# The second Fourier outer product split in seven and moved behind the seventh, in a fused attention and Fourier kernel

## The chip, the cores and the metric

One Trainium2 chip, one core. The metric is the device time of one execution in microseconds, from three runs of each kernel; a profile comes from one further execution. The engines are called PE (TensorE), DVE (VectorE), ACT (ScalarE), POOL (GpSimd) and SP (SyncE, which here only issues transfers).

## The reference

Two independent branches, joined along the last axis: multi-head attention with 32 heads of 32, and a Fourier mixing layer written as matrix products, all in float32.

```python
qkv = (A_x @ wqkv)                                  # 2048 x 1024 by 1024 x 3072, 32 heads
p = softmax(einsum("bhqd,bhkd->bhqk", q, k) * Dh ** -0.5)
a = concat_heads(einsum("bhqk,bhkd->bhqd", p, v)) @ wo
u = einsum("bsd,ed->bse", B_x, dft_hid_re)          # likewise with dft_hid_im
y = einsum("ts,bse->bte", dft_seq_re, u) - einsum("ts,bse->bte", dft_seq_im, u_im)
return concatenate([a, y], axis=-1)
```

## The kernel before

**Products.** Every large product is done by a Strassen-like scheme: operands are cut in quarters, and seven products of sums of quarters replace eight. The products are numbered 1 to 7, and p means such a number. Each operand is kept as a high and a low float32r part (`halves`: a cast at line 549 or 550, a subtraction at line 553), and a pair of 128 x 128 weights and 128 x 512 moving tile takes three matmuls: high by high, low by high, high by low. All of them are recorded at line 433, in `group` (the first ones at line 455).

**Stages.** In program order of these product matmuls: the projections to q, k and v (2016 matmuls); the first Fourier step along the sequence, `dense1` (seven outer products, 2592 here); the second Fourier step, `dense2` (1344); the output projection, `project` (672), which needs all heads.

**The outer products of dense1.** They run in the order `OUTER`, here 1, 2, 5, 6, 7, 4, 3. A plain one (`simple`) has four column blocks n, and for each four row blocks m, and each of the 16 groups adds up 8 pairs: 16 x 8 x 3 = 384 matmuls. Its weights are held for all four n: those of m = 0 and 1 in tiles h and l, those of m = 2 and 3 in slots 16 to 19. A product named in `SPLIT` (here 1 and 3) is itself done in seven inner products, in the order `WITHIN`, by `split`: 7 x 4 groups of 4 pairs, 7 x 4 x 4 x 3 = 336 matmuls. It has more sums of quarters to make (`fetch`: loads at lines 511 and 520, additions at line 530, stores of sums used again at line 538), and it gathers its inner products in accumulators, which lie in slots 16 to 19 (lines 1115 and 1117). `inner` ends its results; for any product but the first, a partial result of another product is loaded (line 1107) and added (line 1141) before the result is stored (line 994, `put_out`). A plain product gathers with a loaded partial result (line 1205) in one instruction at line 986.

**Attention.** Each head has score matmuls psS (line 1586) for the row maxima (DVE, line 1592) and sums (ACT, line 1595), transposed score matmuls psT (line 1711) with an exponential on ACT (line 1718), and the second product P V (line 1741). The maxima's row of a head goes out to DRAM and back by SP (lines 1633 and 1634: m_d, then into qs) before its transposed scores can run.

**What sets the order.** A planner (`Plan`) with costs per operation writes out one fixed order for every engine when the program is built. It hands out product matmuls ("fills") beside attention work: a fill goes when no attention work can, or when its paid share lags behind the attention's done share. Fills of a split product weigh HEAVY = 1.5, and in their stretch (`spare`) ACT may take casts.

```python
        for p in OUTER:
            heavy[0] = HEAVY if p in SPLIT else 1.0
            spare[0] = p in SPLIT
            split(p) if p in SPLIT else simple(p)
```

## Time and profile before

| | us |
|---|---|
| median of three runs | 2923.82 (2922.07 to 2924.57) |
| the profiled execution | 2924.82 |
| its span | 2923.0 |
| TensorE busy | 2911.5 |
| VectorE busy | 2260.2 |
| ScalarE busy | 2297.2 |
| GpSimd busy | 1107.2 |

Times of instructions below are from the profiled execution and counted from the start of its span. A matmul's record lasts longer than its slot (0.39 us), since matmuls overlap; what one costs is the distance between starts. Stretches of outer products are taken by the product matmuls' count in the fixed order: product 1 from 782.2 us, then 2 from 947.8, 5 from 1143.1, 6 from 1340.4, 7 from 1535.6, 4 from 1732.1, 3 from 1928.2, and the second Fourier step from 2108.3 to the end of attention near 2762.2. "x" before a count is the number of instructions; in tables by stretch the columns are stretch, its length, and then for PE, its weight loads, DVE, ACT and POOL the busy time with the count.

### The profile page before, as it was taken

Reading aid. Unit: us, or ns where it says so; the run is one execution under the profiler, and the core shown is the slowest. Engines: PE = TensorE matmul, PEld = TensorE weight load, DVE = VectorE, ACT = ScalarE, POOL = GpSimd, SP = SyncE. Lnnn points to the kernel's source line nnn. Section 1 sums busy time; section 2 is a strip of 40 time slices with the busy share of each in tenths; the row PEclk is TensorE's granted clock in tenths of the full one; section 3 lists DMA queues with packets and bytes.
Section 4 is the critical chain, followed back from the end, with each engine's and each line's share of the span. In section 5 each row is a group of like instructions: output and inputs, shape, how many; then the busy total and the mean of one; then the engine's idle time right before and its main releaser. Section 6 shows DMA issues by size and latency. Waiting matters only on the chain.

```text
span 2923.0 us, 46116 instructions
## 1 busy us (share of the span) xinstructions
PE 2911.5 (100%) x14826; PEld 2130.8 (73%) x14826; DVE 2260.2 (77%) x3072; ACT 2297.2 (79%) x4369; POOL 1107.2 (38%) x866
## 2 busy tenths in 40 slices
PE   9999999999999999999999999999999999999999
PEld 7887777776667776777776777777677777777787
DVE  7778888788889768777778787778877877876496
ACT  5348888888899888888888888988888888887532
POOL 2323335222365124243434342347613653342042
PEclk9999999999999999999999999999999999999999
DMA  9975658766687448678869775568735776663463
GB/s 340 372 241 186 201 183 280 231 214 223 220 263 227 146 136 274 219 241 273 277 224 286 227 240 170 155 192 281 231 98 172 255 238 189 188 189 123 124 241 140
DMA packets 444956, 636.24 MB, mean 218 GB/s; under 512 B 115726, under 2 KB 150286, under 8 KB 444590
## 3 DMA queue, kind: packets, MB, share of 16 engines
q1 hardware_dynamic: 444716, 633.29, 67.8%
q8 instruction: 120, 1.97, 0.3%
q14 instruction: 120, 0.98, 0.1%
HBM read 448.56 MB, written 184.57 MB: 217 GB/s over the span
## 4 chain that ended last, share of the span: by engine, by line
PE 94%; ACT 2%; DMA 2%; DVE 1%; issue 1%; SPq 0%; DVEq 0%; ACTq 0%
PE pd L433 43%; PE psT L1711 16%; PE psS L1586 15%; PE pd L1741 14%; PE psT L433 6%; ACT psS L1595 1%; ACT pt L1718 1%; DMA qs<-m_d 0%; DMA m_d<-lt 0%; DVE negm L1592 0%; DMA raw<-in_ct 0%; PE psT L455 0%; DMA er<-in_xa 0%; DMA qs<-qk_d 0%; DMA er<-in_wv 0%
## 5 line engine op out<-in xcount | busy, mean ns | idle before, releaser
L1592 DVE TENSOR_REDUCE negm<-psS 128x1 f32<-128x1024 f32 x1024 | 1242.4, 1220 | 255.9 <-PE psS L1586 244.6
L1595 ACT ACTIVATE psS<-psS,negm 128x1024 f32<-128x1024 f32 x1024 | 1230.0, 1201 | 75.2 <-DVE negm L1592 69.5
L1718 ACT ACTIVATE pt<-psT 128x512 f32<-128x512 f32 x1656 | 1000.8, 705 | 267.4 <-PE psT L1711 243.8
L433 PE MATMUL pd<-slot,h 128*128 128x512 f32 x2704 | 921.3, 390 | 0.0
L1711 PE MATMUL psT<-qs,ks 128*128 128x512 f32 x2048 | 794.5, 394 | 2.3 <-ACT pt L1718 1.3
L553 POOL TENSOR_TENSOR slot<-raw,slot 128x512 fp32r<-128x512 f32 x278 | 357.6, 1292 | 776.1 <-DVE slot L550 424.2
L433 PEld LDWEIGHTS pd<-slot,h 128*128 128x128 f32 x2704 | 507.5, 188 | 106.1 <-issue 0.8
L530 POOL TENSOR_TENSOR raw<-raw,g 128x512 f32<-128x512 f32 x321 | 414.8, 1302 | 428.4 <-issue 78.1
L433 PE MATMUL pd<-slot,l 128*128 128x512 f32 x1352 | 526.7, 390 | 0.0
L1711 PEld LDWEIGHTS psT<-qs,ks 128*128 128x128 f32 x2048 | 381.9, 188 | 142.0 <-issue 42.7
L1586 PE MATMUL psS<-ks,qs 128*128 128x512 f32 x1552 | 474.0, 391 | 2.5 <-ACT psS L1595 2.2
L433 PE MATMUL pd<-slot,slot 128*128 128x512 f32 x1560 | 436.3, 389 | 0.0
L1741 PE MATMUL pd<-pt,vt 128*32 128x512 f32 x3312 | 408.2, 594 | 0.0
L1586 PEld LDWEIGHTS psS<-ks,qs 128*128 128x128 f32 x1552 | 290.0, 188 | 67.0 <-ACT psS L1595 6.2
L433 PEld LDWEIGHTS pd<-slot,slot 128*128 128x128 f32 x1560 | 292.8, 188 | 60.8
L1595 ACT ACTIVATION_READ_ACCUMULATOR psS<-psS,negm 128x1 f32 x1024 | 328.2, 321 | 0.0
L433 PEld LDWEIGHTS pd<-slot,l 128*128 128x128 f32 x1352 | 253.8, 188 | 52.3
L1718 ACT ACTIVATE ptm<-psT 128x512 f32<-128x512 f32 x392 | 242.4, 716 | 48.9 <-PE psT L1711 47.1
L1741 PEld LDWEIGHTS pd<-pt,vt 128*32 128x32 f32 x3312 | 108.6, 110 | 231.8 <-issue 217.2
L553 POOL TENSOR_TENSOR l<-raw,h 128x512 fp32r<-128x512 f32 x105 | 135.5, 1290 | 224.5 <-PE psT L1711 79.0
L550 DVE CAST slot<-raw 128x512 fp32r<-128x512 f32 x364 | 168.0, 482 | 6.2 <-DMA raw<-in_wo 3.1
L1586 PE MATMUL psS<-ks,qx 128*128 128x512 f32 x496 | 150.1, 393 | 1.0 <-ACT psS L1595 1.0
(158 smaller groups left out, 2066.0 us busy)
## 6 DMA issues: line engine op xcount, KB each, us to landing
raw<-in_ct SPq DMA_DIRECT2D x212, 256.0 KB
g<-in_ct SPq DMA_DIRECT2D x148, 256.0 KB
raw<-ut_d SPq DMA_DIRECT2D x112, 256.0 KB
qk_d<-e SPq DMA_DIRECT2D x52, 512.0 KB
qs<-qk_d SPq DMA_DIRECT2D x128, 192.0 KB
ks<-qk_d SPq DMA_DIRECT2D x128, 192.0 KB
c<-xx_d SPq DMA_DIRECT2D x80, 256.0 KB
c<-u_d SPq DMA_DIRECT2D x72, 256.0 KB
```

Of the source, the lines that this page charges most:

```text
L433: nc.tensor.matmul(box["ps"], a[1]((a[0].hi, a[0].lo)[u]()), b[1]((b[0].hi, b[0].lo)[v]()), start=k == 0, stop=k == n - 1)
L530: return (nc.gpsimd if e == "POOL" else nc.vector).tensor_tensor(out=dest(), in0=x, in1=y, op=ALU.add if sign > 0 and not turned else ALU. ...
L550: return nc.vector.tensor_copy(hi(), raw())
L553: return (nc.gpsimd if e == "POOL" else nc.vector).tensor_tensor(out=lo(), in0=raw(), in1=f(hi()), op=ALU.subtract)
L1586: nc.tensor.matmul(p[:, i * NB : i * NB + NB], (QX[0] if own else QS[h % 2])[:, qt * P : qt * P + P], KS[h % 2][:, c * 1024 + i * NB : c * ...
L1592: nc.vector.tensor_reduce(out=ST["negm"][:, c, qt : qt + 1], in_=box["p"], axis=AX.X, op=ALU.max, negate=True)
L1595: nc.scalar.activation(box["p"], box["p"], AF.Exp, bias=ST["negm"][:, c, qt : qt + 1], accum_out=ST["sums"][:, c, qt : qt + 1])
L1711: nc.tensor.matmul(box["p"], KS[h % 2][:, t * P : t * P + P], QS[h % 2][:, j * NB : j * NB + NB], start=True, stop=True)
L1718: nc.scalar.activation(box["t"], box["p"], AF.Exp)
L1741: nc.tensor.matmul(po["p"][j * DH : j * DH + DH, :], VT[h][:, k, :], box["t"], start=(k == t0), stop=(k == t), tile_position=(0, j * DH),)
```

## The change

The second outer product joins those that are split, and it comes behind the seventh in the order. The constant that tells the planner how many fills there are follows from the length of `SPLIT`.

```diff
@@ -391,7 +391,7 @@
-    SPLIT = (1,3)
+    SPLIT = (1,2,3)
     HEAVY = 1.5
     FILL = 3 * (7 * 24 * 4 + 7 * 16 * 8 - 16 * len(SPLIT) + 7 * 8 * 8 + 2 * 8 * 4)
@@ -1187,7 +1187,7 @@
-    OUTER = (1,2,5,6,7,4,3)
+    OUTER = (1,5,6,7,2,4,3)
     WITHIN = (1, 2, 5, 6, 7, 3, 4)
```

Three places of the fixed order show what moves. The first is PE behind product 7. Before, product 4 begins there: the number behind slot_ names a moving tile, 19472 is the last of the first group's eight, and 19069 is the first again, for the second group (qs and ks belong to scores, pt and ptm to P V).

```order
L433 MATMUL pd<-slot_19472,h 128x512
L1586 MATMUL psS<-ks_333,qx 128x512 x2
L1741 MATMUL pd<-ptm,vt 32x512 x4
L1741 MATMUL pd<-pt,vt 32x512 x23
L1741 MATMUL pd<-ptm,vt 32x512 x5
L1711 MATMUL psT<-qs_2580,ks_2581 128x512 x2
L1586 MATMUL psS<-ks_333,qx 128x512 x4
L1711 MATMUL psT<-qs_2580,ks_2581 128x512
L433 MATMUL pd<-slot_19472,l 128x512
L1711 MATMUL psT<-qs_2580,ks_2581 128x512
L433 MATMUL pd<-slot_19472,h 128x512
L433 MATMUL pd<-slot_19069,h 128x512
```

Now product 2 begins there, and PE's rows at the same turn from the first group to the second are these (17124 and 17171 are the third and fourth of four moving tiles, 17058 the first).

```order
L433 MATMUL pd<-slot_17124,h 128x512
L1586 MATMUL psS<-ks_2601,qs_2600 128x512 x2
L433 MATMUL pd<-slot_17124,l 128x512
L1711 MATMUL psT<-qs_332,ks_333 128x512
L433 MATMUL pd<-slot_17124,h 128x512
L1711 MATMUL psT<-qs_332,ks_333 128x512
L433 MATMUL pd<-slot_17171,h 128x512
L433 MATMUL pd<-slot_17171,l 128x512
L433 MATMUL pd<-slot_17171,h 128x512
L433 MATMUL pd<-slot_17058,h 128x512
L1586 MATMUL psS<-ks_2601,qs_2600 128x512 x2
L1711 MATMUL psT<-qs_332,ks_333 128x512
```

A group there has four pairs instead of eight, and attention's rows stand between them in the same way. The second place is DVE in product 2's stretch. Before, between the maxima of line 1592, it ends one group with one instruction (c is a partial result that was loaded).

```order
L1592 TENSOR_REDUCE negm<-psS 128x1
L986 TENSOR_TENSOR e<-c,pd 128x512
L1592 TENSOR_REDUCE negm<-psS 128x1
L550 CAST slot_11470<-raw 128x512
L553 TENSOR_TENSOR slot_11470<-raw,slot_11470 128x512
L1592 TENSOR_REDUCE negm<-psS 128x1 x3
L986 TENSOR_TENSOR e<-c,pd 128x512
L1592 TENSOR_REDUCE negm<-psS 128x1 x5
L986 TENSOR_TENSOR e<-c,pd 128x512
L1592 TENSOR_REDUCE negm<-psS 128x1
```

Now DVE in product 2's stretch, at its third inner product by WITHIN's numbers 5 and 6 (slot_17596 and slot_18259 are accumulators).

```order
L1592 TENSOR_REDUCE negm<-psS 128x1
L1117 TENSOR_TENSOR slot_17596<-slot_17596,pd 128x512
L1117 TENSOR_TENSOR slot_18259<-slot_18259,pd 128x512
L1592 TENSOR_REDUCE negm<-psS 128x1 x2
L1117 TENSOR_TENSOR slot_17596<-slot_17596,pd 128x512
L1117 TENSOR_TENSOR slot_18259<-slot_18259,pd 128x512
L1592 TENSOR_REDUCE negm<-psS 128x1 x2
L550 CAST slot_18613<-raw 128x512
L550 CAST slot_18618<-raw 128x512
L530 TENSOR_TENSOR raw<-raw,g 128x512
```

One group of such an inner product is added into two accumulators, and more casts stand between the maxima. The third place is SP's queue where the maxima's row of one head goes out (in product 7's stretch before, in product 2's now) (m_d_178, lines 1633 and 1634). Before, stores of results that DVE alone makes stand around it.

```order
L520 DMA g<-in_ct 128x512 x2
L538 DMA s_d_0_372<-raw 128x512
L520 DMA g<-in_ct 128x512
L1633 DMA m_d_178<-lt 4x32x32
L994 DMA ut_d_2_1_314<-e 128x4x128
L994 DMA xx_d_2_7_433<-e 128x512
L1634 DMA qs_332<-m_d_178 2x2048
L1205 DMA c<-xx_d_2_6_464 128x512
```

Now SP has these rows around the same head's row.

```order
L994 DMA ut_d_2_0_305<-e 128x4x128
L1107 DMA c<-xx_d_2_1_414 128x512
L511 DMA raw<-in_xb 128x512
L511 DMA raw<-in_ct 128x512
L994 DMA ut_d_2_0_305<-e 128x4x128
L1107 DMA c<-xx_d_2_1_430 128x512
L511 DMA raw<-in_ct 128x512
L1633 DMA m_d_178<-lt 4x32x32
L520 DMA g<-in_ct 128x512
L1634 DMA qs_332<-m_d_178 2x2048
```

The stores at line 994 are now of the split product's results, which POOL or DVE has first added to a partial result at line 1141, and the loads at line 1107 are those partial results.

## Rows read from the trace of the kernel before

**Rows 1.** The page: span, busy shares by engine, granted clock in 40 slices.
```profile
span 2923.0 us, 46116 instructions
PE 2911.5 (100%) x14826; PEld 2130.8 (73%) x14826; DVE 2260.2 (77%) x3072; ACT 2297.2 (79%) x4369; POOL 1107.2 (38%) x866
...
PEclk9999999999999999999999999999999999999999
```

**Rows 2.** Waits of PE: line waited for, us in total, times, longest.
```profile
PE psS L1586 <- ACT psS L1595: 3.2, 9, 0.6
...
PE psT L1711 <- ACT pt L1718: 1.3, 2, 1.1
PE psT L1711 <- DMA qs<-m_d: 0.8, 2, 0.5
```

**Rows 3.** The page: chain that ended last, shares by engine.
```profile
PE 94%; ACT 2%; DMA 2%; DVE 1%; issue 1%; SPq 0%; DVEq 0%; ACTq 0%
```

**Rows 4.** The chain in order of time: start, us, what; around attention's end.
```profile
2755.22 7.00 PE pd L1741 x64
2762.22 4.53 PE pd L433 x19
...
2769.47 5.44 PE pd L433 x24
```

**Rows 5.** Groups by line and shape: count, busy us, mean ns, idle before by releaser.
```profile
L1718 ACT ACTIVATE pt<-psT 128x512 f32<-128x512 f32 x1656 | 1000.8, 705 | 267.4 <-PE psT L1711 243.8 <-PE pd L1741 23.0
...
L553 POOL TENSOR_TENSOR slot<-raw,slot 128x512 fp32r<-128x512 f32 x278 | 357.6, 1292 | 776.1 <-DVE slot L550 424.2 <-DVE slot L553 72.8 <-PE pd L433 72.6
...
L550 DVE CAST slot<-raw 128x512 fp32r<-128x512 f32 x364 | 168.0, 482 | 6.2 <-DMA raw<-in_wo 3.1 <-POOL raw L530 1.2 <-DMA raw<-in_ct 0.9
...
L553 DVE TENSOR_TENSOR slot<-raw,slot 128x512 fp32r<-128x512 f32 x158 | 113.2, 732 | 8.4 <-ACT slot L549 7.6
...
...
L549 ACT ACTIVATE slot<-raw 128x512 fp32r<-128x512 f32 x72 | 47.8, 686 | 70.5 <-DVE raw L530 24.5 <-PE psT L433 20.3 <-DMA raw<-o_d 18.0
...
L1117 DVE TENSOR_TENSOR slot<-slot,pd 128x512 f32<-128x512 f32 x32 | 21.1, 681 | 3.2 <-PE pd L433 2.8
L1141 POOL TENSOR_TENSOR e<-e,c 128x512 f32<-128x512 f32 x15 | 19.4, 1294 | 8.6 <-DVE slot L550 7.8 <-DVE e L990 0.7
```

**Rows 6.** By stretch, all engines: products 1, 2, 5, 6, 7, 4, 3, dense2.
```profile
782.20:947.80 165.60, 164.44 (x840) 118.69 (x839) 145.07 (x208) 151.72 (x293) 105.83 (x84) 1.00 0.78 242
947.80:1143.10 195.30, 195.02 (x1019) 140.01 (x1018) 143.85 (x190) 165.10 (x319) 48.68 (x38) 1.00 0.57 172
1143.10:1340.40 197.30, 197.19 (x1030) 142.31 (x1029) 145.69 (x191) 169.20 (x326) 76.78 (x61) 1.00 0.72 232
1340.40:1535.60 195.20, 194.71 (x1021) 140.71 (x1020) 151.13 (x204) 166.04 (x320) 75.04 (x60) 1.00 0.82 266
1535.60:1732.10 196.50, 195.73 (x1021) 140.06 (x1020) 157.22 (x205) 166.40 (x319) 75.23 (x58) 1.00 0.79 248
1732.10:1928.20 196.10, 196.10 (x1026) 141.85 (x1026) 146.35 (x197) 169.04 (x326) 53.72 (x42) 1.00 0.57 171
1928.20:2108.30 180.10, 178.77 (x941) 125.34 (x941) 151.47 (x208) 158.13 (x306) 118.91 (x94) 1.00 0.81 254
2108.30:2762.20 653.90, 653.06 (x3418) 467.69 (x3416) 478.35 (x667) 530.22 (x1016) 247.79 (x194) 1.00 0.57 174
```

**Rows 7.** The same, P V (line 1741) on PE alone; products 1 and 2.
```profile
782.20:947.80 165.60, 26.79 (x240) 1.00 0.78 242
947.80:1143.10 195.30, 35.37 (x320) 1.00 0.57 172
```

**Rows 8.** The chain's shares by line in the stretches of products 4 and 3.
```profile
by line: PE pd L433 44.3%; PE psT L1711 19.3%; PE psS L1586 18.6%; PE pd L1741 17.9%
...
by line: PE pd L433 34.7%; PE pd L1741 19.4%; PE psS L1586 15.5%; PE psT L1711 15.0%; ACT psS L1595 8.7%; ACT pt L1718 4.3%; issue 1.6%; DVE negm L1592 0.7%; ACT ptm L1718 0.2%; DVE lh L1622 0.1%; DVE tt L1648 0.1%
```

**Rows 9.** Waits of the SP queue in product 3's stretch: us, times, longest.
```profile
SPq L994 <- POOL e L1141: 17.7, 9, 6.8
```

## Prediction

> **What bounds the kernel now.** I read the page's busy shares first, then who TensorE waited for, then the chain of waits, then tables by stretch. TensorE is busy 2911.5 of 2923.0 us, at the full granted clock in every slice [rows 1]. Busy time of matmuls is modelled, so three other views have to confirm it. Its waits: the longest group is 3.2 us in 9 waits, and behind it, beside start-up, come 1.3 and 0.8 us [rows 2]. The chain that ended last is 94% TensorE [rows 3]. And in order of time 24 matmuls of a product take 5.44 us, so one is worth 5.44/24 = 0.2267 us from start to start; 64 records of the second attention product (P V) take 7.00 us, 0.1094 us each [rows 4]. With these prices the content of the whole program is known: 6624 product matmuls and 2 x 2048 score matmuls at 0.2267, 4096 P V records at 0.1094, which is 1501.7 + 928.6 + 448.1 = 2878 us. Only 2923 - 2878 = 45 us is anything else, start and end included. So the kernel is bound by the number of its matmuls, and a matmul taken out is worth nearly its whole slot, unless the work that replaces it makes TensorE wait.
>
> The attention of the 32 heads and the Fourier products are interleaved on TensorE; only when the last head is done can the output projection begin. The last P V starts at 2755.22 us and 19 matmuls of the last Fourier step follow it at 2762.22 [rows 4]; then comes the projection.
>
> **What the change removes.** A plain outer product is 16 groups of 8 chunk pairs with 3 matmuls each, 384; one split in seven is 7 x 4 groups of 4 pairs, 336. The order agrees: 6552 rows of line 433 before, 6504 now, and 2048 of each attention kind in both; the runs of P V matmuls are 72 in both. That is 48 matmuls x 0.2267 = **10.9 us** of TensorE.
>
> By the Trainium skill (TensorE: Matmul & The Clock Gate, Back-to-back issue gap) such matmuls in a stream of weight loads and matmuls come 131 ns apart, and the 48 would be worth 6.3 us. The trace has 227 ns for one, over stretches of 24, and the measurement decides.
>
> **What it adds, beside TensorE.** The order has 20 more accumulations on DVE at lines 1115 and 1117 (0.68 us: 13.6 us), 13 more casts there (0.48: 6.3) and 13 more additions and subtractions (0.73: 9.5); 17 more casts on ACT (0.69: 11.7); on POOL 32 more at line 530, 25 at line 553 and 17 at line 1141 (1.29 each, as at the last two: 95.5 us); and 90 more transfers of 256 KB on SP's queue, 23 MB more beside 633 [rows 5]. The product's stretch is where this must fit. In the plain second product's stretch DVE is busy 143.85 of 195.3 us, ACT 165.10, POOL 48.68; in the third, already split, DVE 151.47 of 180.1, ACT 158.13, POOL 118.91 [rows 6]. So all of it fits: POOL has 61 us left there, DVE 28 and ACT 22. I cost it at nothing as busy time. Its cover is the stream of score and product matmuls; if DVE had to carry a further 28 us in that stretch, the maxima of the scores would come late and TensorE would wait for the score banks.
>
> **What it costs TensorE in waits.** This price can be read, since two products are split already. From each stretch of [rows 6] I take the content: its matmul count less the P V records at 0.2267, plus those (240 in product 1's and 320 in each of the others, [rows 7]) at 0.1094. Product 1 (split): 600 and 240, 162.3 us, and 165.6 were spent: 3.3 over. Product 3 (split): 621 and 320, 175.8 of 180.1: 4.3 over. The plain ones: product 2, 193.5 of 195.3, 1.8; product 5, 196.0 of 197.3, 1.3; product 6, 193.9 of 195.2, 1.3; product 7, 193.9 of 196.5, 2.6; product 4, 195.1 of 196.1, 1.0. The plain mean is 1.6 (part of it is the turn to P V and back). So splitting costs 3.3 - 1.6 = 1.7 us after product 1's pattern and 4.3 - 1.6 = **2.7 us** after product 3's. I take the latter, the nearer row: the new one, like product 3, adds a stored partial result on POOL behind each of its 16 final results (line 1141), which product 1 does not. The chain shows where it comes from: in product 3's stretch 8.7% and 4.3% of it run over ACT's two exponentials, in product 4's stretch it is all TensorE [rows 8].
>
> The moves. Product 5 now follows a split product, as product 2 did. Product 4 does so too, and there the held weights of its third and fourth row blocks (slots 16 to 19) can only be written when the accumulators in the same slots are read out for the last time. The first two row blocks, 48 matmuls among attention work, stand ahead and hide that. The only such row is product 2 with 1.8 over, beside 1.3 for product 5: **0.5 us** more, since now two products stand there rather than one. The other scatter among plain products, 1.0 to 2.6, has no cause that I can name, and I carry it as the error. The tail is unchanged in the order: 19 product matmuls behind the last P V in both programs, and the projection of 672 matmuls.
>
> **Sum.** -10.9 + 2.7 + 0.5 = -7.7 us. The profiled execution took 2924.82 us around a span of 2923.0, so 1.8 lie around the span and it was 1.0 above the median of the three runs, 2923.82. The span becomes 2915.3, that execution would be 2917.1, and the median 2916.1, 0.26% less. About 0.2%, 5.8 us, is what a measurement of this kernel can tell from no change. The surcharge may be between nothing (then the 10.9 stands whole: 2912.9; a gain from the new order itself I limit to the plain stretches' scatter) and double product 3's (5.4).
>
> **Rivals.**
> *Two split products near each other cost double.* Products 2 and 3 now have one plain product between them. If POOL's and ACT's backlogs pass over, each shows another surcharge: 2.7 + 2.7 + 0.5 = 5.9 against 10.9, so -5.0 and 2918.8, too little to be told from nothing. For it: the chain over ACT in product 3's stretch [rows 8]. Against: product 4's stretch between them is the quietest of all, POOL 53.72 of 196.1 us busy and 1.0 over content [rows 6].
>
> *TensorE has room, and the freed slots stay empty.* Then the end of attention is set by the engines beside it (ACT 79% busy, [rows 1]), the Fourier work is only done earlier, and the projection begins when it began: 2923.8, no change. Against: TensorE hardly waits for anybody [rows 2], ACT's idle time is mostly waiting for score matmuls, 243.8 us at line 1718 [rows 5], and the order still has Fourier matmuls up to the last P V. The Trainium skill speaks for this rival (Perfetto Trace Analysis, Identifying the Most-Contended Engine): it calls matmul busy time a poor measure and asks for the weight loads' busy share. That is 73% here [rows 1], which would leave a quarter of TensorE free; the back-to-back starts of [rows 4] contradict it.
>
> *The SP queue holds up a head.* Each result of the new product is stored from SP's queue behind POOL's addition, and the queue stands while it waits: 17.7 us in 9 waits, up to 6.8, in product 3's stretch [rows 9]. In the order the row of a head's maxima (lines 1633 and 1634), for which its transposed score matmuls wait, stands right behind such stores in the new stretch, where the order before has stores that wait for DVE alone. TensorE waited only 0.8 us on it so far [rows 2]. If all 17.7 us fell on head starts, the sum would be -10.9 + 2.7 + 0.5 + 17.7 = +10.0, or 2933.8. It turns to a loss once 7.7 us of it reaches TensorE.
>
> That the change does not do what it says is excluded by the order's counts.
>
> **How the numbers follow.** Forecast 2916.1: 0.75, since the price of a matmul and the price of a split stretch are both read from this program. Double cost, 2918.8: 0.14. TensorE has room, 2923.8: 0.06. The SP queue, 2933.8: 0.05. The forecast's own scatter is two or three stretches' error of about 0.6 us each and the bound of no surcharge: 2912.5 to 2918.5. The range reaches over the double cost and its scatter, 2912.5 to 2920.5, and leaves out the last two rivals and tails, less than 2 in 10. Faster by over 0.2% (under 2918.0): nearly all of the forecast and a little of the double cost, 0.75. Within: the rest of the double cost, the idle slots and a little of the forecast, 0.20. Slower: 0.05.
>
> **What would show it.** Right: 6576 product matmuls; the second product's stretch, now behind the seventh, some 3 to 5 us over its content; the plain ones at 1 to 2.6; the last P V about 8 us earlier, and 161 us from its end to the end of the span, as before. Wrong: TensorE waiting several us for score banks or for the maxima's row there; a stretch of attention alone before the projection; or a last Fourier step (653.9 us to the end of P V [rows 6]) that loses what the middle gained.

## The result: 13 us slower, not 8 us faster

The changed kernel takes 2937.54 us (median of six runs, 2935.38 to 2940.68); the kernel before, run beside it, 2924.36 (2922.07 to 2926.24). The ratio is 1.0046, 95% interval 1.0033 to 1.0059: 13.2 us slower. The forecast was 2916.1 with a range up to 2920.5, and the case "slower" had a chance of 0.05.

The profiled execution of the changed kernel took 2935.39 us around a span of 2933.3, 10.3 longer than the span before; it is one of the two fastest of the six, 2.2 us under their median, and the account below is of these 10.3 us. Its page, to be held against [rows 1] and [rows 3]:

```profile
span 2933.3 us, 46343 instructions
PE 2908.6 (99%) x14778; PEld 2118.1 (72%) x14778; DVE 2293.1 (78%) x3119; ACT 2308.3 (79%) x4386; POOL 1199.0 (41%) x938
...
PE 89%; DMA 4%; ACT 3%; DVE 2%; SPq 1%; issue 1%; POOL 0%; DVEq 0%; ACTq 0%; POOLq 0%
PE pd L433 40%; PE psT L1711 15%; PE psS L1586 14%; PE pd L1741 13%; PE psT L433 6%; ACT psS L1595 2%; DMA raw<-in_ct 2%; ACT pt L1718 1%; DVE negm L1592 1%; DMA raw<-in_xb 1%; DMA m_d<-lt 0%; DMA qs<-qk_d 0%; DMA er<-in_xa 0%; SPq L324 0%; DMA raw<-w_d 0%
```

The 48 matmuls are gone (14826 to 14778), but TensorE's share of the chain that ended last fell from 94% to 89%. What came in is transfers (DMA from 2% to 4%), ACT and DVE. Two inputs of the Fourier branch stand out among the transfers: in_ct, whose tiles become moving tiles, and in_xb, whose tiles become weights ("loads of c" and "loads of x" below; a sum of x that is stored is s, one of c is t). TensorE's busy time fell by only 2.9 us and its idle time rose from 2923.0 - 2911.5 = 11.5 to 2933.3 - 2908.6 = 24.7 us. Whom it waited for (us in total, times, longest), to be held against [rows 2]:

```profile
PE psS L1586 <- ACT psS L1595: 7.6, 16, 1.2
PE psT L1711 <- ACT pt L1718: 3.3, 3, 1.7
PE pd L433 <- DMA raw<-in_xb: 2.5, 1, 2.5
...
PE psT L1711 <- DMA qs<-m_d: 1.7, 3, 1.1
```

The score banks (line 1586), 3.2 us before, cost 7.6 now. Next the table by stretch (window, length, then busy time and count of PE, weight loads, DVE, ACT, POOL; granted clock, DMA share, GB/s), in the new order 1, 5, 6, 7, 2, 4, 3, dense2, against [rows 6]:

```profile
783.30:949.40 166.10, 164.38 (x840) 118.67 (x839) 144.57 (x204) 151.93 (x293) 109.43 (x86) 1.00 0.80 253
949.40:1151.80 202.40, 198.00 (x1026) 140.59 (x1026) 156.75 (x205) 168.93 (x325) 82.92 (x65) 1.00 0.81 262
1151.80:1348.30 196.50, 196.50 (x1025) 141.18 (x1024) 150.95 (x200) 167.45 (x323) 78.72 (x63) 1.00 0.78 256
1348.30:1544.40 196.10, 195.14 (x1016) 138.50 (x1015) 150.50 (x199) 165.39 (x317) 76.39 (x60) 1.00 0.77 246
1544.40:1731.20 186.80, 181.93 (x951) 125.69 (x950) 161.54 (x220) 160.88 (x311) 116.40 (x93) 1.00 0.84 260
1731.20:1931.10 199.90, 199.19 (x1032) 142.39 (x1031) 149.34 (x205) 172.10 (x333) 66.95 (x53) 1.00 0.59 175
1931.10:2101.20 170.10, 167.34 (x860) 119.46 (x859) 150.95 (x201) 150.10 (x290) 110.98 (x88) 1.00 0.86 266
2101.20:2776.70 675.50, 673.63 (x3537) 481.06 (x3536) 501.39 (x685) 549.75 (x1052) 252.37 (x196) 1.00 0.56 171
```

Two columns matter. The first is the length against the content, worked out as in the prediction (P V records of the changed kernel: 240 in product 1, 256 in product 3, 1152 in dense2, 320 in the other products; dense2 goes to its last product matmul here). Product 5: 706 x 0.2267 + 320 x 0.1094 = 195.1, and 202.4 were spent, 7.3 over. The same for every stretch, and for the kernels of the experiments, in us over content (an s marks a split product; "q, k, v" is all from the first product matmul of the program to product 1, and the projection ends with TensorE's last matmul, so the sum before is 31.4 and not the prediction's 45):

| stretch | before | after | move alone | split alone |
|---|---|---|---|---|
| q, k, v | 9.3 | 10.4 | 10.1 | 10.9 |
| 1s | 3.1 | 3.8 | 2.9 | 2.5 |
| 5 | 1.3 | 7.3 | 7.2 | 11.9 |
| 6 | 1.3 | 1.7 | 1.3 | 3.8 |
| 7 | 2.6 | 3.3 | 2.3 | 1.2 |
| 2 | 1.6 | 8.7 (s) | 1.0 | 5.1 (s) |
| 4 | 1.0 | 3.5 | 0.8 | 4.3 |
| 3s | 4.3 | 5.2 | 4.8 | 4.6 |
| dense2 | 6.8 | 8.8 | 8.3 | 11.8 |
| projection | 0.1 | -0.1 | 0 | 7.9 |
| sum | 31.4 | 52.6 | 38.6 | 64.0 |

Content fell by 10.9, waits rose by 52.6 - 31.4 = 21.2, and 21.2 - 10.9 = 10.3 is the longer span. Of the 21.2 the profile shows 13.2 as idle time of TensorE; the rest are starts further apart than 0.2267 us whose rows, 0.39 us long, leave no gap. Two stretches carry most of it: product 5, 6.0 more, and product 2 with product 4 behind it, 9.6 more.

The second column is the last. Before, the rates ran 242, **172**, 232, 266, 248, 171, 254 GB/s: behind the split product 1 came a light stretch. Now they run 253, 262, 256, 246, 260, 175, 266: five full ones in a row.

The last P V begins at 2765.59 instead of 2755.22, 10.4 us later, and the rest is as it was [rows 4]. Chain in order of time:

```profile
2765.59 7.00 PE pd L1741 x64
...
2779.84 5.44 PE pd L433 x24
```

### The profile page after: what moved, and what is told of

Read it like the earlier page. It is cut to its first block, busy times and chain, and to the rows that moved or that the text cites. A ratio compares the mean times of both kernels' runs of the same rounds, so it can differ in the third digit from the quotient of the medians.

```text
span 2933.3 us, 46343 instructions
## 1 busy us (share of the span) xinstructions
PE 2908.6 (99%) x14778; PEld 2118.1 (72%) x14778; DVE 2293.1 (78%) x3119; ACT 2308.3 (79%) x4386; POOL 1199.0 (41%) x938
## 4 chain that ended last, share of the span: by engine, by line
PE 89%; DMA 4%; ACT 3%; DVE 2%; SPq 1%; issue 1%; POOL 0%; DVEq 0%; ACTq 0%; POOLq 0%
PE pd L433 40%; PE psT L1711 15%; PE psS L1586 14%; PE pd L1741 13%; PE psT L433 6%; ACT psS L1595 2%; DMA raw<-in_ct 2%; ACT pt L1718 1%; DVE negm L1592 1%; DMA raw<-in_xb 1%; DMA m_d<-lt 0%; DMA qs<-qk_d 0%; DMA er<-in_xa 0%; SPq L324 0%; DMA raw<-w_d 0%
## 5 line engine op out<-in xcount | busy, mean ns | idle before, releaser
L433 PE MATMUL pd<-slot,h 128*128 128x512 f32 x2800 | 956.2, 390 | 0.0
L553 POOL TENSOR_TENSOR slot<-raw,slot 128x512 fp32r<-128x512 f32 x290 | 373.4, 1294 | 672.1 <-DVE slot L550 359.7
L530 POOL TENSOR_TENSOR raw<-raw,g 128x512 f32<-128x512 f32 x353 | 456.7, 1303 | 409.5 <-DMA raw<-in_ct 77.5
L433 PEld LDWEIGHTS pd<-slot,h 128*128 128x128 f32 x2800 | 525.5, 188 | 108.7 <-issue 0.8
L433 PE MATMUL pd<-slot,l 128*128 128x512 f32 x1400 | 545.7, 390 | 2.5 <-DMA raw<-in_xb 2.5
L433 PE MATMUL pd<-slot,slot 128*128 128x512 f32 x1368 | 379.8, 389 | 0.0
L433 PEld LDWEIGHTS pd<-slot,l 128*128 128x128 f32 x1400 | 262.8, 188 | 56.9 <-POOL l L553 2.8
L433 PEld LDWEIGHTS pd<-slot,slot 128*128 128x128 f32 x1368 | 256.8, 188 | 53.2
L553 POOL TENSOR_TENSOR l<-raw,h 128x512 fp32r<-128x512 f32 x118 | 152.4, 1291 | 260.7 <-DVE h L550 90.3
L550 DVE CAST slot<-raw 128x512 fp32r<-128x512 f32 x375 | 187.7, 522 | 7.9 <-POOL raw L530 4.0
```

The source lines that it names most:

```text
L433: nc.tensor.matmul(box["ps"], a[1]((a[0].hi, a[0].lo)[u]()), b[1]((b[0].hi, b[0].lo)[v]()), start=k == 0, stop=k == n - 1)
L530: return (nc.gpsimd if e == "POOL" else nc.vector).tensor_tensor(out=dest(), in0=x, in1=y, op=ALU.add if sign > 0 and not turned else ALU. ...
L550: return nc.vector.tensor_copy(hi(), raw())
L553: return (nc.gpsimd if e == "POOL" else nc.vector).tensor_tensor(out=lo(), in0=raw(), in1=f(hi()), op=ALU.subtract)
```

## The experiments

The expectations give the theories letters. A is first that the move costs the time, then, more closely, that transfers do which land late where they are dense; B that the split does, wherever it stands; C and C' that the planner's figures for a transfer are wrong; D that the added work on DVE, ACT and POOL costs it; E that any new order of the same work does; F that casts on ACT do. They give products 5 and 2 of the changed kernel as 7.7 and 9.2 us over content, counted a matmul or two less than in the table (7.3 and 8.7). A difference in us is always to the kernel before, run beside it.

### The move alone and the split alone

The kernel before with one line changed each:

```diff
-    OUTER = (1,2,5,6,7,4,3)
+    OUTER = (1,5,6,7,2,4,3)
```

> The order of the changed kernel (1, 5, 6, 7, 2, 4, 3) with only products 1 and 3 split, as before: the move alone, matmuls as before. Theory A (the move did it: the plain second product, the light stretch of 172 GB/s behind split product 1, is gone, product 5 with its sums and stores stands there and its loads come late): product 5's stretch again 6 to 8 us over its content instead of 1.3, and 2929 to 2932 us in all against 2924. Theory B (splitting the second product did it, wherever it stands): 2923 to 2926, product 5's stretch 1 to 3 over.

```diff
-    SPLIT = (1,3)
+    SPLIT = (1,2,3)
```

> Products 1, 2 and 3 split in the order of the kernel before (1, 2, 5, 6, 7, 4, 3): the split alone, 48 matmuls fewer. Theory A (the move did it): the split keeps most of its 10.9 us, its own stretch 4 to 6 us over, 2915 to 2922; but if what counts is that a light stretch follows a split one, product 5 still stands behind a split one here and 6 us more are lost, 2922 to 2928. Theory B (the split did it, wherever it stands, 21 us of waits against 10.9 saved): 2934 to 2939.

The move alone: 2933.0, ratio 1.003 (1.0019 to 1.0041), +9.0 us with no matmul less. The split alone, in the old order: 2945.67, 1.0072 (1.0057 to 1.0087), +21.6, beyond what either theory had expected. Both: +13.2. So the move pays for itself only beside the split (21.6 to 13.2), the split costs 4.2 more than the move alone even in its new place (less than two plans of the same work can differ, see below), and the kernel before beats all three. The table above says where: the move's loss lies in product 5 (7.2) whether product 2 is split or not, and moving product 2 behind product 7 puts that loss on product 5 because it now stands behind the split product 1.

What product 5 meets there shows in a short window. The transfers of the first 70 us behind product 1 (packets, MB, share of the 16 DMA engines): before, where product 2 stands there, in the changed kernel, and with the move alone.

```profile
q1 hardware_dynamic: 10002, 10.55, 51.2%
```

```profile
q1 hardware_dynamic: 14173, 21.66, 96.1%
```

```profile
q1 hardware_dynamic: 14327, 21.92, 94.4%
```

Twice the bytes of before, on DMA engines that are busy nearly throughout. Product 5 stores 40 sums that product 6 uses, and loads and adds tiles for itself. In slices of 20 us of the changed kernel (columns as above) the loss ends with this congestion:

```profile
949.40:969.40 20.00, 19.25 (x115) 11.02 (x114) 15.63 (x24) 12.11 (x24) 9.41 (x8) 1.00 0.95 296
969.40:989.40 20.00, 17.98 (x79) 14.97 (x80) 18.49 (x22) 18.96 (x37) 12.20 (x10) 1.00 0.99 311
...
1009.40:1029.40 20.00, 18.82 (x82) 14.46 (x81) 17.24 (x18) 18.33 (x36) 14.95 (x12) 1.00 0.95 309
1029.40:1049.40 20.00, 20.00 (x122) 12.39 (x121) 12.77 (x22) 14.29 (x28) 1.29 (x1) 1.00 0.66 213
```

How a late tile reaches TensorE, in the chain of the changed kernel:

```profile
1001.57 6.09 DMA raw<-in_ct
...
1007.78 1.30 POOL raw L530
...
1009.11 1.50 DVE slot L550
1010.61 1.15 DVE negm L1592
...
1012.14 1.21 ACT psS L1595 x2
...
1013.39 0.74 PE psS L1586 x2
```

The load of a 256 KB tile takes 6.09 us. POOL adds, and DVE's cast waits for POOL. The order on DVE is fixed, so the maxima of the scores (negm) stand behind that cast, the exponential on ACT behind the maxima, and TensorE's next scores behind the exponential, which frees their bank. Two of these steps are slow: the load (the last section has one of 3.25 us), and the cast, which takes 1.50 us where its kind takes 0.42 and runs beside a subtraction of POOL, from 1009.02 for 1.31 us. The casts of line 550 into slots take 522 ns in the mean now and 482 before [rows 5]; what that alone costs TensorE was not tested. At product 5's start it is direct: the load of x lands late and the first product matmul waits 2.5 us for it (the third of the waits above). SP's queue doesn't stand longer than before: its longest groups of waits in product 5's stretch are 24.7 us at line 994, 12.0 at line 538 and 11.8 at line 511, and 28.6, 19.2 and 12.2 in product 5's stretch before; for stores of t that still hold a buffer it waits 5.8 us, 5.2 before.

### What of product 5 does it: stores, transfers, additions, or the split product ahead

First the changed kernel without product 5's 40 stores of sums (keep_a and keep_b no longer hold product 5, and product 6 takes input tiles in their place, so the result is another):

```diff
-                return split_a(p, q, (s1_d[m][k], s1[m][k]), (s2_d[m][k], s2[m][k]))
+                return split_a(p, q, q(1, 0), (s2_d[m][k], s2[m][k]))
...
-            keep_a = {5: lambda m, k: (s1_d[m][k], s1[m][k]), 6: lambda m, k: (s2_d[m][k], s2[m][k])}.get(p, lambda m, k: None)
+            keep_a = {6: lambda m, k: (s2_d[m][k], s2[m][k])}.get(p, lambda m, k: None)
...
```

> The changed kernel, but product 5 does not store its 40 sums of 256 KB, and product 6 loads 40 input tiles in their place (so the result is another; every addition, load, cast and matmul is there). Theory A (behind a split product, product 5's dense transfers land late and hold what stands behind them): product 5's stretch falls from 7.7 to 2 to 4 us over its content, 2931 to 2934 in all against 2937.5. Theory D (product 5's additions and casts, on top of what the split product left over on DVE, ACT and POOL, hold it): no change, 2936 to 2940.

2928.88, ratio 1.0018 (1.0008 to 1.0027), +4.9 instead of +13.2. Its product 5:

```profile
947.50:1144.80 197.30, 197.15 (x1026) 141.40 (x1026) 151.39 (x202) 168.14 (x325) 86.79 (x68) 1.00 0.72 222
```

The same 1026 matmuls, 2.2 over content instead of 7.3, with as many additions (POOL 86.79 us, even more than 82.92). In its first 70 us the DMA share is 83.7%. The run further below that leaves out product 2's stores as well repeats it, with 2.6 over.

Second the other way round, the kernel before with 64 transfers of 256 KB between buffers in DRAM, two behind each moving tile of product 2; nothing is added on POOL, DVE or ACT:

```diff
...
+                        for r in range(2 if p == 2 else 0):
+                            op("SP", ISSUE, lambda n=n, c=c, r=r: nc.sync.dma_start(spill[n, c, r], ct[1, 8 * r + c, :, n * NB : n * NB + NB]), [M[-1].made[0]], [], seq(), 256)
```

> The kernel before with 64 more transfers of 256 KB, DRAM to DRAM, tied to product 2's tiles and read by nobody: the transfers alone, with no work for the other engines. Theory A: product 2's stretch, behind split product 1, rises from 2 us over its content to 5 to 9, and the whole to 2927 to 2932. Theory D: 2923 to 2926.

Third the same number of additions instead, in place on tiles that have been read, without a transfer:

```diff
...
+        for _ in range(extra):
+            last = op("POOL", SUB, lambda e: (nc.gpsimd if e == "POOL" else nc.vector).tensor_tensor(out=raw(), in0=raw(), in1=raw(), op=ALU.add),
+                      [last], [users], seq(), other=("DVE", ADD, 20 + seq()), two=True)
...
-                        M.append(moving((8 * z + c) % 12, b(n, c), keep_b(n, c)))
+                        M.append(moving((8 * z + c) % 12, b(n, c), keep_b(n, c), None, 2 if p == 2 else 0))
```

> The kernel before with 64 more additions of 128 x 512 in product 2's stretch, in place on tiles that are read already, for POOL or DVE as the planner has it: the work of the change's 74 POOL operations without its transfers. Theory A: product 2's stretch stays within 2 us of its 1.8 over content, 2923 to 2927 in all, beside 2938 for 64 more transfers in the same place. Theory D: 5 us over or more, 2928 or more.

Product 2 in each, behind the split product 1, transfers first and additions second:

```profile
947.50:1156.90 209.40, 200.57 (x1020) 143.18 (x1018) 145.25 (x195) 166.21 (x319) 42.75 (x34) 0.98 0.80 236
```

```profile
949.10:1144.40 195.30, 194.99 (x1019) 139.65 (x1018) 156.97 (x215) 164.32 (x317) 89.00 (x76) 1.00 0.56 172
```

The transfers: 15.7 us over content instead of 1.6, total 2938.32, ratio 1.005 (1.0033 to 1.0067), +14.4, more than expected. Of the 15.7, 8.8 are idle time, and some 4 may be put down to the granted clock, 0.98 over this stretch (the last section has such a fall). The 64 issues also take time of SP's queue, and the chain of this run passes through them at product 2's start; how much of the loss is the queue's isn't separated. The additions: 1.8 over, with DVE at 156.97 and POOL at 89.00 us, both above product 5's in the changed kernel. So in this place it is not the engines' work but the transfers. The additions' kernel is slower all the same, 2935.96, 1.004 (1.0025 to 1.0055), +10.6, which by the total alone is theory D's range; but the loss lies in product 3's stretch, whose work is unchanged: 12.8 over instead of 4.3. Scatter of the plan, which comes below, can do such a thing; that it did here isn't shown.

Fourth the changed kernel with product 1 plain:

```diff
-    SPLIT = (1,2,3)
+    SPLIT = (2,3)
```

> The changed order (1, 5, 6, 7, 2, 4, 3) with products 2 and 3 split and product 1 plain: as many matmuls as before the change. Theory A (what hurts is product 5 directly behind a split product): product 5's stretch falls from 7.7 to 1 to 3 us over its content, product 2's stays at 5 to 9 over, 2926 to 2931 in all. If product 5 is slow wherever it comes second: it stays at 7 to 8 over, and 2932 to 2937 in all.

Product 5, with its 40 stores, is 0.9 over now, at a DMA share of 84.1% in its first 70 us:

```profile
974.30:1170.70 196.40, 196.40 (x1028) 142.04 (x1027) 143.43 (x187) 168.38 (x325) 76.32 (x61) 1.00 0.71 231
```

So both are needed, a split product ahead and the stores; either alone costs nearly nothing. The DMA issues of the 70 us ahead of product 5 suggest why. Behind the plain product 1 of this kernel, at a share of 58.4%, its work on tiles of x has begun (loads of x, and at last stores of its sums of x):

```profile
raw<-in_xb SPq DMA_DIRECT2D x7, 256.0 KB
...
g<-in_xb SPq DMA_DIRECT2D x6, 256.0 KB
...
s_d<-raw SPq DMA_DIRECT2D x4, 256.0 KB
```

Behind the split product 1 of the changed kernel, at 79.3%, there is less of it in the same time:

```profile
raw<-in_xb SPq DMA_DIRECT2D x5, 256.0 KB
...
g<-in_xb SPq DMA_DIRECT2D x2, 256.0 KB
s_d<-raw SPq DMA_DIRECT2D x2, 256.0 KB
```

7 loads of x instead of 13; with the move alone it is 7 too, and in the kernel before, where product 5 stands behind the plain product 2, 13. In the 70 us behind product 5's start in the changed kernel 12 more such loads and 6 stores follow, on top of its loads of c and its stores of t. (The names don't tell which product each load serves; the stores of s are product 5's.) Before, product 5 moved 19.66 MB in its first 70 us at 87.7%, and its whole stretch was 1.3 over. So the reading is that a split product leaves less room to fetch ahead for the next, and what is not fetched ahead meets the next one's own transfers.

The DMA share by itself doesn't decide it. Over product 5's first 70 us it goes with the loss: 83.7% without the stores (2.2 over), 84.1% behind the plain product 1 (0.9), 87.7% before (1.3), 94.4% with the move alone (7.2), 96.1% in the changed kernel (7.3), 99.7% with the split alone (11.9). But in the first 70 us of product 6 in the kernel before, the engines move even more:

```profile
q1 hardware_dynamic: 14590, 22.42, 96.7%
```

Product 6 is 1.3 over there, with no wait of TensorE in those 70 us. No tile of x or s is loaded in them; 13 such loads stand in the 70 us ahead. That fits the reading: what costs is a load that is needed soon and comes late, not the bytes as such.

In total the kernel with product 1 plain is no better, 2935.6, 1.0038 (1.0025 to 1.0051), +11.7, with as many matmuls as before: products 2 (4.7), 4 (6.0), 3 (8.2) and dense2 (10.4) lose instead, so the total is not what theory A expected, though product 5 is.

### The split product's own price

In the changed kernel product 2 is 8.7 over, where 1 would be usual for a plain one there (1.0 with the move alone). First, ACT's share. The casts that the split products may hand to ACT are taken away for product 2:

```diff
-            spare[0] = p in SPLIT
+            spare[0] = p in SPLIT and p != 2
```

> The changed kernel, but in product 2's stretch ACT may not take casts (DVE takes them): ACT's queue, in which the exponentials stand, never waits for a landing there. Theory F (casts on ACT that wait for late landings hold the exponentials, 4.6 us of ACT's waits in that stretch): product 2's stretch falls from 9.2 to 5 to 6 us over its content, 2932 to 2936 in all. Theory A without F: 8 to 10 us over, 2936 to 2943.

2942.82, 1.0067 (1.0052 to 1.0082), +18.5; product 2 is again 8.7 over. 24 casts go from ACT to DVE, and ACT's added casts are not the cause.

Second, product 5's 40 stores and product 2's own 20 stores of sums are left out (input tiles in place of what was stored, so the result is another):

```diff
-                            M[n, c] = moving((8 * z + 4 * n + c) % 12, split_b(j, q, at(5, n, c), at(6, n, c)), at(j, n, c) if j in (5, 6) else None)
+                            M[n, c] = moving((8 * z + 4 * n + c) % 12, split_b(j, q, *((q(0, 1), q(1, 1)) if i == 2 else (at(5, n, c), at(6, n, c)))), at(j, n, c) if j in (5, 6) and i != 2 else None)
...
```

> The run that left out product 5's stores of sums (product 6 loading input tiles in their place), and split product 2 does not store its 20 sums either and loads input tiles in their place (the result is another; all additions, casts and matmuls are there). Theory A (transfers, dense over a long stretch): product 2's stretch falls from 8 to 9 us over its content to 4 to 6, 2921 to 2927 in all against 2929. Theory D (split product 2's work on DVE, ACT and POOL): 2927 to 2931 as without it.

2930.44, 1.0016 (1.0006 to 1.0025), +5.1: nothing beyond what product 5's stores gave (+4.9). Product 2 is 6.7 over, against 7.8 with those alone. Its stores are worth about 1 us at most, which is where theory D, not A, had expected this run.

Third, the sums of product 2 with their loads and stores are left out (single quarters instead of sums, 60 transfers and 40 additions less; the result is another):

```diff
-                    A.append(piece(split_a(j, lambda r, k: base_a(2 * r + n, k), at(5, n), at(6, n)), at(j, n) if j in (5, 6) else None))
+                    qa = lambda r, k: base_a(2 * r + n, k)
+                    A.append(piece([(1, *qa(j % 2, n))], None) if i == 2 else piece(split_a(j, qa, at(5, n), at(6, n)), at(j, n) if j in (5, 6) else None))
...
-                            M[n, c] = moving((8 * z + 4 * n + c) % 12, split_b(j, q, at(5, n, c), at(6, n, c)), at(j, n, c) if j in (5, 6) else None)
+                            M[n, c] = moving((8 * z + 4 * n + c) % 12, [(1, *q(j % 2, n))] if i == 2 else split_b(j, q, at(5, n, c), at(6, n, c)), at(j, n, c) if j in (5, 6) and i != 2 else None)
```

> The changed kernel, but split product 2 uses single input quarters in place of sums of two, and stores no sums (the result is another): some 60 fewer transfers of 256 KB in its stretch and 40 fewer additions, all casts, accumulations, partial results and matmuls there. Theory A: its stretch falls from 9.2 to 3 to 5 us over its content, and the one behind it (product 4) from 3.7 to 1 to 2, 2927 to 2932 in all. If not the transfers but the casts, the accumulations or the SP queue's stores of the 16 results hold it: still 7 to 10 over, 2935 to 2940.

Products 2 and 4 here:

```profile
1542.10:1709.60 167.50, 166.25 (x860) 120.28 (x859) 141.86 (x198) 147.39 (x287) 82.83 (x66) 1.00 0.63 194
1709.60:1906.90 197.30, 196.75 (x1028) 141.64 (x1027) 148.40 (x199) 168.77 (x327) 65.47 (x52) 1.00 0.57 169
```

256 P V records lie in the first. Product 2 is 2.6 over, product 4 1.8 (8.7 and 3.5 in the changed kernel); DMA share 0.63 instead of 0.84. So the sums with their transfers are the split product's price and most of what product 4 loses behind it. The total is 2933.73, 1.0035 (1.0025 to 1.0046), +9.4: product 5's 7.6 is there as in the changed kernel, and another 8.1 is lost in the projection, where 64 P V records were left behind when the last Fourier step had run out.

Whether it is the transfers of these sums or their additions that costs, inside the split product itself, these runs don't separate. For the transfers speaks the chain of the changed kernel in this stretch, which runs over a sum's load and another's store (6.78 and 5.92 us), loads of c and x (6.40 and 4.92) and a head's q (4.79); against them, that the stores alone were worth so little. The slices are not as clear as in product 5:

```profile
1584.40:1604.40 20.00, 20.00 (x122) 12.49 (x121) 17.53 (x29) 16.00 (x32) 8.91 (x7) 1.00 0.91 280
1604.40:1624.40 20.00, 19.28 (x85) 15.26 (x84) 15.73 (x20) 18.81 (x38) 13.52 (x11) 1.00 0.98 294
1624.40:1644.40 20.00, 18.82 (x115) 10.70 (x114) 18.86 (x23) 14.77 (x29) 12.58 (x11) 1.00 0.93 300
...
1664.40:1684.40 20.00, 18.20 (x112) 10.38 (x112) 15.77 (x31) 15.37 (x31) 7.06 (x7) 1.00 0.89 266
```

One slice at 0.91 loses nothing, one at 0.89 loses 1.8 us: here too the share alone doesn't say whether TensorE pays.

### How much of it is the plan's scatter

Every edit makes the planner write another order. Two of its constants, changed by next to nothing, show what that alone does: the cost of a DVE evacuation (h1) and the lateness that it grants (h2), each in both kernels.

```diff
-    MAX, EVAC, CAST, BIT = 1.22, 0.685, 0.415, 0.275
+    MAX, EVAC, CAST, BIT = 1.22, 0.700, 0.415, 0.275
```

> The kernel before with one cost of the planner moved by a hair (accumulation on DVE 0.700 us instead of 0.685): the same work and the same products, another fixed order. Theory E (a new fixed order of the same work by itself loses some us against the one in the kernel before, wherever the stalls fall): 2927 to 2935. Theory A (the move and the split are what costs): 2922 to 2926.

> The changed kernel with the same hair's breadth (0.700 instead of 0.685). Theory E: anywhere from 2924 to 2945, with the stalls in other stretches than products 5 and 2. Theory A: 2934 to 2940, with product 5's stretch 6 to 9 and product 2's 5 to 9 us over their content again.

```diff
-    LATE = 0.15
+    LATE = 0.17
```

> The kernel before with another hair's breadth (the planner's wait before it counts work as ready, LATE, 0.17 us instead of 0.15). Theory E: 2927 to 2935. Theory A: 2922 to 2926.

> The changed kernel with LATE 0.17 instead of 0.15. Theory E: 2924 to 2945, stalls in other stretches. Theory A: 2934 to 2940, products 5 and 2 again 6 to 9 and 5 to 9 us over their content.

| | before | changed | difference |
|---|---|---|---|
| as it is | 2924.36 | 2937.54 | 13.2 |
| evacuation 0.700 | 2927.27 | 2943.71 | 16.4 |
| lateness 0.17 | 2930.47 | 2942.05 | 11.6 |

Another order of the same work costs the kernel before 1.9 (ratio 1.0006, 0.9997 to 1.0015) and 5.1 us (1.0018, 1.0009 to 1.0028), and the changed one 5.2 and 3.5 (against the kernel before, run beside each, +18.4 and +16.7 instead of +13.2). By their totals all four runs lie in theory E's ranges and outside theory A's. But the change loses 11.6 to 16.4 in every pair, so a loss is systematic, and its own product 2 shows 8.6 to 9.1 over in three plans of it and with ACT's casts taken away. Product 5 there has 7.3, 5.1 and 12.1. Where the rest falls differs: of the 16.4, some 9 lie in the projection, for which 64 P V records were left over. A difference under some 5 us between two plans is no finding here; a loss in a stretch whose work is unchanged (12.8 and 10.8 in product 3) may be nothing else.

### The planner's figures

If the planner only misjudges how long a transfer takes, longer figures should repair the changed kernel. Its landing time and its rate were changed in both kernels, and its reserve of instructions on each engine in the changed one:

```diff
-    LANDING = 1.6
+    LANDING = 4.0
```

> The changed kernel with one number of the planner changed: it takes a transfer to land 4.0 us after its data instead of 1.6. Theory C (transfers land later than planned where they are dense, and instructions stand in the fixed order of DVE and ACT too early for them, so that the score work behind them is held): the stretches of products 5 and 2 fall from 7.7 and 9.2 us over their content to 2 to 4, 2925 to 2930 in all. If late landings are not the cause: 2935 to 2940 as the changed kernel.

> The kernel before with the same number changed (landing 4.0 us instead of 1.6): the control for the run of the changed kernel with that number. Theory C: little to gain, 2921 to 2925, since the stretches there lose 1 to 4 us only. If the number itself does something else (weights taken later, fills moved), it shows here as a change of the same size as in the changed kernel.

```diff
-    KB_US = 360.0
+    KB_US = 290.0
```

> The changed kernel with the planner's rate for transfers lowered from 360 to 290 KB per us, near the 311 GB/s at which the DMA engines were 96% busy from 950 to 1020 us. Theory C' (the plan hands out transfers faster than they can run, so they land late and the fixed order is wrong by some us): the plan now has them where they land, the waits in products 5 and 2 shrink by half or more, 2924 to 2931. If the transfers cost their time however they are planned: 2934 to 2941.

> The kernel before with the same rate in the planner (290 instead of 360): the control. Theory C': 2919 to 2924, a little better in its split stretches. If the rate only shifts work about: 2924 to 2930.

```diff
-    MARGIN = {"POOL": 2, "DVE": 2, "ACT": 0}
+    MARGIN = {"POOL": 4, "DVE": 4, "ACT": 3}
...
-        pl.MARGIN["DVE"] = 3 if heads and t_on[0] else 2
+        pl.MARGIN["DVE"] = 5 if heads and t_on[0] else 4
```

> The changed kernel with the planner's margin behind a landing raised from 2 (3 during attention) to 4 (5) us for DVE and from 2 to 4 for POOL, and from 0 to 3 us for ACT: work that needs a landed tile stands later in the order of those engines. Theory C (instructions that wait for late landings hold the score work queued behind them on DVE and ACT): TensorE's waits for score banks and exponentials shrink, 2926 to 2933 in all. If the landings do not act in this way: 2935 to 2942.

Landing 4.0: 2986.82 changed (ratio 1.0214), 2979.0 before (1.0188). Rate 290: 2977.57 (1.0179) and 2968.25 (1.0147). Reserve: 2944.12 (1.0069). All miss. The first two lose 35 to 41 us ahead of the first product instead of 9 to 10, and 9 to 21 in the projection, alike in both kernels, so their totals say nothing of the stretches in question. In the stretches themselves product 5 of the changed kernel is still 7.0 over with the landing and 6.3 with the rate (1.6 and 1.2 in the kernel before), product 2 11.1 and 6.3. With the reserve product 5 is 6.6 and product 2 6.7 over. None of the three takes product 5's loss away. Whether a planner with a better model of congestion would keep the 10.9 us is open.

No version that was run beats the kernel before.

## Why the prediction was wrong

- **The matmuls.** Right. 48 went, and the content fell by 10.9 us by the same working. TensorE was the bound: 24 product matmuls take 5.44 us in both kernels.
- **"I cost it at nothing as busy time."** This is where it failed first. As busy time of DVE, ACT and POOL it was right: 64 additions in the plain product behind product 1 cost nothing there (1.8 over instead of 1.6). But the list of what is added ends with 90 more transfers, and for these the prediction looked at SP's queue alone, never at the 16 DMA engines or at when a load lands, though the last two columns of [rows 6] show how full they are. Product 2's new stretch has a DMA share of 0.84 instead of 0.57; without its sums, 60 transfers and 40 additions, it is 2.6 over instead of 8.7. A load that lands late comes through POOL, DVE and ACT to the score banks. The prediction had named that way ("the maxima of the scores would come late"), but tied it to DVE's own load.
- **"2.7" for splitting.** In the prediction's own reckoning it measured 8.7 - 1.6 = 7.1. It was read from product 3, whose neighbours are light on transfers (171 and 174 GB/s in [rows 6]), so its surcharge is one with room on both sides; that this is why it was too small is a reading. Even product 3's own is not fixed: 3.5 to 12.8 over the plans of this study.
- **"0.5" for the moves.** It measured 8.5: 6.0 in product 5 and 2.5 in product 4, the two that now stand behind a split product. 5.9 of product 5's come with the move alone, whose 70 us behind product 1 are at 94% where they were at 51%; product 4's come with the sums of the split product ahead (1.8 over without them, 3.5 with). The step took product 2's 1.8 as the price of standing behind a split product. But product 2 stores no sums and moves 172 GB/s over its stretch; product 5 moves 232 [rows 6]. The nearest row was of the wrong kind: product 2 was the light stretch in which tiles for product 5 were fetched ahead.
- **The sum.** -10.9 + 7.1 + 8.5 = 4.7, and the other stretches lose 5.6 more, none of them over 2.0, each within scatter: 10.3 for the span, where the sum had -7.7.
- **The rivals.** "Two split products cost double" pointed the right way, but had 5.9 for all waits, where they rose by 21.2; and it argued with POOL's and ACT's backlog, not the transfers'. "TensorE has room" is false: it has 72% of its time in weight loads, and still 21.2 us of waits less 10.9 of content made the span 10.3 longer. "The SP queue holds up a head" had the right sign, and 2933.8 was near by chance, since its mechanism is not what the trace shows: in product 2's stretch SP waited for POOL's sums (line 1141) 8.4 us in 10 waits, none over 1.6, and TensorE waited 1.7 us in the whole program for the maxima's row, nowhere in that stretch.

```profile
SPq L994 <- POOL e L1141: 8.4, 10, 1.6
```

- **What would show it.** The last P V came 10.4 us later rather than 8 earlier, with the same 161 us behind it; three of the plain products are over 2.6, one by far (product 5), two by a little (4 and 7). The condition "TensorE waiting several us for score banks" came true in product 2's stretch:

```profile
PE psS L1586 <- ACT psS L1595: 3.1, 5, 1.2
```

  Product 5's stretch, where the prediction did not look, adds 1.6 of the 7.6 us, beside its 2.5 for a load of x.

The chance of 0.05 for slower was too small for a reason that could be seen ahead: the sum had a gain known to 0.1 us and two prices each read from one or two stretches, with another neighbourhood than the new one.

## What to carry to other kernels

Where TensorE is the bound, a matmul taken out is worth its slot, and the question is only what the work that replaces it does to everybody's loads. The DMA engines' share in windows of some 70 us around each move shows where to look (whole stretches, at 0.57 and 0.81, hid 51% and 96%), but not what it costs: 97% cost product 6 nothing. What the loads of such a window are for, and how many of them could have gone ahead, must be looked at too. A light stretch between heavy ones may be what keeps the heavy ones cheap, and moving it costs although no work is added; a price read from one neighbourhood holds for that neighbourhood. And where a planner writes the order anew at every edit, nudge a constant in both kernels before a difference of a few microseconds is believed.

## What the runs showed of the hardware

**A transfer's time under load.** In the chain of the changed kernel five of the six loads of 256 KB at product 5's start take 4.79 to 6.09 us and one 2.83, where the 16 DMA engines are 95% to 100% busy and move 296 to 347 GB/s. In order of time (start, us, what), and behind them one at a lighter time, where the share is 0.53 and the rate 167 GB/s (another, in product 1's stretch, takes 5.39 us at a share of 0.81):

```profile
958.43 5.20 DMA r_d<-ll
...
963.73 4.79 DMA raw<-in_xb
...
968.59 2.83 DMA raw<-in_xb
...
2024.99 3.25 DMA raw<-in_ct
```

The first is a store of 16 KB, and it takes as long as a load of 256.

**A wait can cost more than its length.** In the kernel with 64 more transfers TensorE waits 2.90 us for a score bank, and then its matmuls start 0.43 us apart instead of 0.23 for some 2.5 us. PE in order of time (start, us, then the idle time ahead in brackets), and two windows behind it (the clock is the third from the end):

```profile
1068.05 1.22 PE L1589 MATMUL psS<-ks,qs 128*128 128x512 f32 x2 [2.90 <-ACT psS L1598]
1069.07 0.63 PE L1714 MATMUL psT<-qs,ks 128*128 128x512 f32 x1
1069.50 0.63 PE L433 MATMUL pd<-slot,h 128*128 128x512 f32 x1
```

```profile
1070.00:1071.00 1.00, 1.00 (x4) 0.81 (x3) 0.97 (x3) 0.97 (x3) 0.00 (x0) 0.50 1.00 322
...
1072.00:1073.00 1.00, 1.00 (x6) 0.79 (x5) 0.73 (x1) 0.78 (x4) 0.00 (x0) 1.00 0.85 145
```

The granted clock is at its lower level, 1.2 GHz, around the end of the wait, and back at 2.4 GHz in the window from 1072. The length of the wait alone doesn't tell whether this happens. In the profiled execution of the changed kernel, where the longest wait is 2.5 us, the clock stays at 1.00 in every stretch; with the split alone a wait of 1.7 us for an exponential, in product 4's stretch, is followed by a clock of 0.50 from 1925 to 1927 us.
